# A different table of ordering offsets for the instruction streams of a two-layer attention and feed-forward kernel

## The chip, the core and the metric

The kernel runs on one core of one Trainium2 chip. The metric is the device time of one execution in microseconds (us), the median of three runs. One profiled execution of the kernel before is at hand too, with a trace of every instruction. TensorE is PE below (its weight loads PEld), VectorE is DVE, ScalarE is ACT, GpSimd is POOL, and SyncE, which issues most DMAs, is SP.

## What is computed

The input x has 2048 rows (tokens) of 640 numbers in bf16. Four residual steps follow one another: attention layer A, feed-forward layer B, and the same two again with the same weights.

```python
def _A_ref(x, wq, wk, wv, wo, beta):          # H=32 heads of Dh=20, N=4 segments of L=512 rows
    q, k, v = x @ wq, x @ wk, x @ wv          # cut into heads and segments
    phi = lambda t: jnp.where(t > 0, t + 1.0, jnp.exp(t))
    g = _sigmoid(beta).reshape(1, H, 1, 1)
    M, z = 0, 0                               # memory, one matrix and one vector per head
    for s in range(N):
        logits = jnp.einsum('bhqd,bhkd->bhqk', qs, ks) * scale + mask      # causal in the segment
        a_dot = jnp.einsum('bhqk,bhkd->bhqd', _softmax(logits), vs)
        num = jnp.einsum('bhld,bhde->bhle', phi(qs), M)
        den = jnp.einsum('bhld,bhd->bhl', phi(qs), z)[..., None] + 1e-06
        outs.append(g * num / den + (1.0 - g) * a_dot)
        M = M + jnp.einsum('bhld,bhle->bhde', phi(ks), vs)
        z = z + jnp.einsum('bhld->bhd', phi(ks))
    return concat(outs) @ wo

def _B_ref(x, w1, w2):                        # w1 640 x 1728, w2 1728 x 640
    return jnp.maximum(x @ w1, 0) @ w2

x = x + _A_ref(_layernorm(x), wq, wk, wv, wo, beta)
x = x + _B_ref(_layernorm(x), w1, w2)
x = x + _A_ref(_layernorm(x), wq, wk, wv, wo, beta)
x = x + _B_ref(_layernorm(x), w1, w2)
```

## The kernel before

**Tiling.** x stays on chip as 16 blocks of 128 rows (`x_sb`). All work goes by segments of four such blocks, eight in all: four of the first pass through A and B, called phases 0 to 3 below, and four of the second, phases 4 to 7. In each segment a layer norm by DVE and POOL (statistics L785 and L787, the power -1/2 L801, normalization L831) writes `xn_tok`; a DMA transposes it into `xnT` (`turn`, L804, issued at L807). PE multiplies `xnT` with wq, wk and wv (`proj_one`, `proj_v`), five products of contraction 128 for each output of 128 x 512 or 128 x 320. The helper `group` gives each product in two forms: one matmul over the whole array (L764) or four matmuls of 32 columns each, quarters (L767). The planner picks the form by the tiling that PE is in.

The sums in PSUM (`ps`) are copied out by ACT or DVE, whichever the planner finds free sooner (`evac`, L491; `settle`, L971 on DVE and L972 on ACT for q and k). q and k (`stg`) are then spilled to HBM (`spill`, L1060, `scr`) and read back with four heads spread over the array's rows (`fill`, L1109, `pad`). Scores (L1293) run in rounds of small matmuls on four row groups, ACT takes the exponential of each 128 x 1024 result (L1357), POOL masks the diagonal blocks (L1369), and PE applies the result to v in four column groups (`apply`, L1389), whose output is copied out at L1399 (`otu`) and transposed to `otk` by DMA. `phi_` (L1136 on DVE, L1138 on ACT, L1139 on DVE) computes phi(q) and phi(k) from `stg` once the block is spilled, into `phs`; `turn_k` transposes phi(k) by DMA (`phk`); `mem_write` multiplies it with v (L1230, again as full matmuls or as quarters, the latter with only the columns of the heads that the quarter holds, except in the first of each group). `out_proj` multiplies with wo and adds to x (L1511), `ln_b` is the second layer norm, `ffn` multiplies with w1, applies the relu (L1586 on DVE, L1587 on ACT), multiplies with w2 and adds to x (`residual`, L1606); `ffn_rest` (L1564) does the 64 columns of w1 that don't fill a block. `late_loads` brings in the weights for the first pass and later parts of x (L641) on SP.

**Order.** Nothing here is ordered by hand. The work is written as 39 generators, called streams, each of which yields its instructions in its own order, such as `scores` (number 0), `spill` (13), `turn_k` (19), `mem_write` (20), `proj_one` (29 and 30), `ffn` (32) and `late_loads` (38). A planner (`Sched.run`) keeps a model of when every engine is free and when every result is there. At each step it looks at the next instruction of each stream and records the one with the least key. Each engine, and SP's DMA queue with it, later executes its instructions in the recorded order, with waits on semaphores for what they depend on. The key is (L407):

```python
key = (round(start + late + SHIFT.get(self.place(n, st[1]), 0)),
       0.5 if op.urgent else prio, self.rank[id(st[1])], n)
```

`start` is the modelled start in ns. `late` (`_late`, L348) adds what a PE instruction would be short of a fixed distance behind what it waits for, once the first score rounds are done: 400 ns behind another engine, 1000 ns behind a DMA's landing. `SHIFT` is a table of offsets in ns, and `place` (L260) says which entry holds:

```python
def place(self, n, gen):
    k = self.made.get(id(gen), 0)
    return n, self.phase.get(id(gen), 0), sum(k >= x for x in (6, 20, 60))
```

An entry's name is thus the number of the stream, the phase that it is in (0 to 7), and how many instructions it has recorded in that phase: 0 for under 6, 1 for under 20, 2 for under 60, 3 beyond. A negative offset makes the planner record the instruction earlier than its modelled start, a positive one later. Offsets change the order in which instructions of different streams are recorded. With the order can change which engine copies a sum out, and which form a product has, since both are picked when it is recorded. An order in which a DMA is recorded earlier on SP also moves whatever stands behind it: SP waits in order, for example in `turn` until the block has been written, and in `fill` until the spilled block has landed.

## Time and profile before

| what | value |
|---|---|
| median of three runs | 552.99 us (550.38, 552.99, 553.38) |
| the profiled execution | 550.77 us, of which the span of instructions 548.3 us |
| PE busy | 540.1 us, 99%, 10283 matmuls |
| DVE, ACT, POOL busy | 424.7 us, 409.9 us, 196.8 us |
| granted TensorE clock | 1.0 |
| HBM traffic | 20.57 MB read, 12.85 MB written |

The span runs from the first to the last instruction of the profiled execution; the time around it is 2.5 us. An engine's busy time is the sum over its instructions, without waits. L12 means line 12 of the kernel; in `group`, `turn` and other helpers all callers share a line and are told apart by their operands. In a row of the trace that lists instructions in order, the first number is the start in us from the span's start, the second the time until the last of the xN instructions in that row ended, and a bracket gives the idle time before it with what ended it. `SPq` is SP's DMA queue, where the second number is the time for issuing.

### The profile page before, as it was taken

To read this page: it belongs to the slowest core of one execution; us is meant where nothing else is said; L and a number is where in the kernel's file an instruction comes from. 1 tells how busy PE (TensorE), PEld (TensorE's weight loads), DVE (VectorE), ACT (ScalarE), POOL (GpSimd) and SP (SyncE) were. 2 spreads that over 40 slices of the span, in tenths; PEclk is the share of its full clock that TensorE was granted. 3 is DMA by queue.
4 is the path that set the end of the run, shared out by engine and by line. 5 is a ranking of instruction groups with operands and counts; after the bars stand their busy time and mean duration, and the time that the engine had idled before them with its cause. 6 is when DMAs were issued, how large, how long until landed. Compare 5 with 4: busy or idle time off the path is not lost.

```text
span 548.3 us, 22987 instructions
## 1 busy us (share of the span) xinstructions
PE 540.1 (99%) x10283; PEld 309.9 (57%) x10283; DVE 424.7 (77%) x1060; ACT 409.9 (75%) x522; POOL 196.8 (36%) x305
## 2 busy tenths in 40 slices
PE   8999999999999999999999999999999999999997
PEld 7434465455554555545465554665456655657766
DVE  4999898798889789987798887989688877637102
ACT  6899979899878898788888878886787776551140
POOL 2655533343444334343344444334333322301000
PEclk9999999999999999999999999999999999999999
DMA  8799789845635326375384614571265611340401
GB/s 272 189 231 259 162 179 203 222 86 105 164 83 89 78 39 163 78 114 77 115 144 114 110 31 140 115 126 26 52 179 102 122 34 28 80 83 15 88 4 51
DMA packets 133476, 62.36 MB, mean 114 GB/s; under 512 B 112258, under 2 KB 123266, under 8 KB 133378
## 3 DMA queue, kind: packets, MB, share of 16 engines
q1 hardware_dynamic: 132832, 60.38, 50.8%
q8 instruction: 81, 1.33, 1.0%
q10 hardware_dynamic: 546, 0.52, 0.3%
q14 instruction: 17, 0.14, 0.1%
HBM read 20.57 MB, written 12.85 MB: 61 GB/s over the span
## 4 chain that ended last, share of the span: by engine, by line
PE 89%; DVE 4%; DMA 4%; POOL 1%; ACT 1%; SPq 1%; issue 1%
PE ps L767 48%; PE ps L764 22%; PE ps L1293 9%; PE ps L1389 6%; PE ps L1172 2%; DMA scr<-stg 1%; DMA x_sb<-in_A_x_dram 1%; PE ps L1230 1%; DMA otk<-otu 1%; PE ps L1564 1%; ACT PT L1357 1%; DVE stats L785 1%; POOL PT L1369 1%; SPq L615 0%; POOL rstd L801 0%
## 5 line engine op out<-in xcount | busy, mean ns | idle before, releaser
L1357 ACT ACTIVATE PT<-ps 128x1024 bf16<-128x1024 f32 x320 | 309.3, 1023 | 61.6 <-PE ps L1293 57.6
L1369 POOL TENSOR_SCALAR_AFFINE_SELECT PT<-PT 128x512 bf16<-128x512 bf16 x256 | 169.9, 681 | 247.6 <-ACT PT L1357 247.6
L767 PE MATMUL ps<-xnT,w_r 128*32 128x512 bf16 x1856 | 110.9, 379 | 0.0
L767 PE MATMUL ps<-w_r,hT 128*32 128x320 bf16 (+1 forms) x1876 | 72.7, 295 | 0.0
L767 PEld LDWEIGHTS ps<-xnT,w_r 128*32 128x32 bf16 x1856 | 46.7, 97 | 44.6 <-issue 5.0
L1293 PE MATMUL ps<-pad 20*128 20x512 bf16 (+3 forms) x1024 | 63.3, 301 | 0.0
L764 PE MATMUL ps<-w_r,hT 128*128 128x320 bf16 x376 | 60.3, 300 | 0.0
L1606 DVE TENSOR_TENSOR x_sb<-x_sb,ps 128x320 bf16<-128x320 bf16 (+1 forms) x65 | 30.7, 475 | 37.8 <-PE ps L767 35.6
L785 DVE BATCH_NORM_STATS2 stats<-x_sb 128x6 f32<-128x320 bf16 x124 | 55.2, 474 | 3.9 <-DMA x_sb<-in_A_x_dram 3.3
L767 PEld LDWEIGHTS ps<-w_r,hT 128*32 128x32 bf16 x1876 | 47.9, 97 | 12.4 <-issue 1.6
L1293 PEld LDWEIGHTS ps<-pad 20*128 20x128 bf16 x1024 | 17.8, 92 | 51.1 <-issue 25.0
L764 PEld LDWEIGHTS ps<-w_r,hT 128*128 128x128 bf16 x376 | 34.7, 98 | 17.5 <-issue 5.0
L1587 ACT ACTIVATE hT<-ps 128x512 bf16<-128x512 f32 x52 | 31.1, 598 | 17.9 <-PE ps L767 17.3
L1586 DVE TENSOR_SCALAR hT<-ps 128x512 bf16<-128x512 f32 x52 | 35.3, 680 | 11.7 <-PE ps L767 9.0
L1511 DVE TENSOR_TENSOR x_sb<-x_sb,ps 128x320 bf16<-128x320 bf16 x64 | 30.1, 478 | 15.5 <-PE ps L767 12.1
L801 POOL TENSOR_TENSOR rstd<-lnU,mhalf 128x2 f32<-128x2 f32 (+2 forms) x27 | 21.0, 778 | 56.2 <-DVE lnU L797 42.8
L1389 PE MATMUL ps<-PT,v_aug 128*21 128x128 bf16 (+3 forms) x896 | 40.3, 300 | 0.0
L1399 DVE CAST otu<-ps 128x512 bf16<-128x512 f32 x50 | 34.1, 683 | 7.9 <-PE ps L1389 7.6
L971 DVE CAST stg<-ps 128x512 bf16<-128x512 f32 x42 | 28.5, 683 | 8.4 <-PE ps L767 7.1
L1483 DVE TENSOR_TENSOR o_sb<-otk,rden 128x320 bf16<-128x320 bf16 x62 | 33.9, 571 | 0.6
L831 DVE TENSOR_SCALAR xn_tok<-x_sb,mv,rstd 128x640 bf16<-128x640 bf16 x60 | 29.8, 519 | 3.4 <-POOL rstd L801 3.4
L1138 ACT ACTIVATE stg<-stg 128x512 bf16<-128x512 bf16 x50 | 31.6, 631 | 0.4 <-DVE rtmp L1136 0.4
(113 smaller groups left out, 706.7 us busy)
## 6 DMA issues: line engine op xcount, KB each, us to landing
pad<-scr SPq DMA_DIRECT2D x124, 80.0 KB
scr<-stg SPq DMA_DIRECT2D x34, 256.0 KB, 2.6
out_dram<-x_sb SPq DMA_DIRECT2D x15, 160.0 KB, 2.2
w_r<-in_B_w_dram SPq DMA_DIRECT2D x10, 216.0 KB, 3.8
w_r<-in_B_w_dram SPq DMA_DIRECT2D x13, 160.0 KB, 2.9
x_sb<-in_A_x_dram SPq DMA_DIRECT2D x10, 160.0 KB, 3.3
scr<-w_r SPq DMA_DIRECT2D x5, 256.0 KB, 4.0
wv_r<-in_A_wv_dram SPq DMA_DIRECT2D x1, 800.0 KB, 7.7
```

What stands on the lines that cost most here:

```text
L764: return e.matmul(view(dst.ap, b), a, b, start=(k == 0), stop=(k == last))
L767: return e.matmul(view(dst.ap[rows], b), part, b, start=(k == 0), stop=(k == last))
L785: tk = yield dve(320, 1, lambda e, c2=c2: e.bn_stats(stats6[:, t, c2, :], x_sb[:, t, c2 * 320:(c2 + 1) * 320]), xt)
L1138: te = yield act(512, lambda e, q=q: e.activation(q, q, ACT.Exp), [tr] + p, psum=False)
L1293: fns.append([(lambda e, z=z, j=j, hh=hh, N=N, o=o, sl=sl, q=hh % 2: e.matmul(slot.ap[:, q, o:o + N], sl.ap[32 * hh:32 * hh + DH, z, 0, 12 ...
L1357: tx = yield act(1024, lambda e, dst=dst, src=src: e.activation(dst, src, ACT.Exp, scale=SCALE), sc + pw)
L1369: tm = yield pool(600.0, lambda e, reg=reg: e.affine_select(out=reg, in_=reg, pattern=[[0, 4], [1, 128]], compare_op=ALU.is_ge, fill=0.0, ...
L1389: fns.append((lambda e, OD, j=j, hh=hh: e.matmul(OD.ap[32 * hh:32 * hh + DH + 1, 128 * j:L], VAUG[vx(a, s)][:, j, 4 * g + hh, :], pt.ap[:, ...
L1399: te = yield evac(L, 1, lambda e: e.tensor_copy(dst, OD.ap), lambda e: e.activation(dst, OD.ap, ACT.Copy), [tk] + OTU[0].tks)
L1483: to = yield dve(320, 1, lambda e, z=z, dst=dst: e.tensor_tensor(dst, av[:, z, :, :, 0:DH], rd.ap[:, z].to_broadcast([128, NJ, 4, DH]), AL ...
L1586: th = yield evac(512, 1, lambda e: e.tensor_scalar(hT[:, dc, :], bk.ap[:, :], 0.0, None, ALU.max), lambda e: e.activation(hT[:, dc, :], b ...
L1587: lambda e: e.activation(hT[:, dc, :], bk.ap[:, :], ACT.Relu), [tk] + HT.tks)
```

## The change

The table `SHIFT` is replaced; nothing else differs. It had 265 entries and has 278. 201 names are in both, 10 of them with the same value. Instructions, tiles, buffers, transfers and the planner's rules stay, so that every difference between the two kernels is one of order, of the form of a product (full or quarters) or of the engine that copies a sum out of PSUM. The new table came out of a search over the planner's model in which landing times of DMAs were varied. The lines behind the table have numbers higher by two afterwards. Of the diff, the entries of some streams follow, with the values before and after (a dash is no entry, which counts as 0):

```
stream (number)      (phase, count): before -> after
causal (2)           (0,0): -100 -> -700   (0,1): -663 -> -700   (0,2): -1075 -> -700   (1,0): 400 -> 4050   ...
turn_pair (5)        (0,0): -5225 -> -6362   (1,0): 500 -> -1500   (3,0): -1988 -> -6000   ...
out_proj (8, 9)      (8,7,0): 3000 -> 200   (8,7,1): 3500 -> -   (8,7,2): 3000 -> 100   (9,7,0..2): 1000 -> -50   ...
fill (12)            (1,0): 2274 -> 1462   (2,0): 5175 -> -50   (2,1): -3537 -> -50   ...
spill (13)           (0,0): -888 -> -400   (1,0): 200 -> -   (2,0): 7413 -> 4300   (3,0): -50 -> 425   ...
turn_k (19)          (0,0): 500 -> -200   (1,0): - -> -200   (2,0): 500 -> -   (5,0): -3850 -> -400   ...
mem_write (20)       (2,0): -200 -> -100   (4,1): 225 -> -900   (6,1): -700 -> -1600   ...
proj_first (28)      (0,0): 475 -> -850   (0,1): -400 -> 50   (0,2): -200 -> -
proj_v (31)          (1,1): -6000 -> -875   (2,0): - -> -2500   (7,1): -5350 -> -   (7,2): - -> -2000   ...
ffn (32)             (7,0): 100 -> 3000   (7,1): -7500 -> 3000   (7,2): -7500 -> 3000   (7,3): 500 -> 2925   ...
late_loads (38)      (0,0): -12 -> -   (0,1): 175 -> -100   (0,2): 3087 -> 2400
```

and as lines of the code, shortened:

```diff
 SHIFT = {
-    (0, 0, 0): -12, (0, 1, 1): -26, (0, 2, 0): -50, (0, 3, 0): -50, (1, 0, 0): -312, (1, 0, 1): -1663,
...
+    (37, 0, 0): 300, (37, 0, 1): 2250, (38, 0, 1): -100, (38, 0, 2): 2400,
 }
```

## The prediction

> **What bounds the kernel now.** I read the page first, then PE's busy time by stretches, then who PE waited for, then single rows in order of time.

> ```profile
> span 548.3 us, 22987 instructions
> PE 540.1 (99%) x10283; PEld 309.9 (57%) x10283; DVE 424.7 (77%) x1060; ACT 409.9 (75%) x522; POOL 196.8 (36%) x305
> ```

> TensorE is the bound: 540.1 of 548.3 us. The next view splits the span into stretches (columns: length, then busy time and instructions of each engine, granted clock, DMA share).

> ```profile
> 0.00:27.40 27.40, 24.54 (x220) 16.75 (x221) 19.60 (x57) 19.38 (x40) 12.50 (x31) 1.00 0.82 231
> 27.40:54.80 27.40, 25.05 (x390) 10.69 (x388) 25.94 (x60) 25.98 (x29) 14.37 (x23) 1.00 0.97 245
> 82.20:520.90 438.70, 438.70 (x8739) 250.20 (x8740) 350.17 (x865) 335.49 (x414) 157.73 (x234) 1.00 0.48 100
> 520.90:548.30 27.40, 24.55 (x680) 17.12 (x668) 4.05 (x9) 5.61 (x10) 0.00 (x0) 1.00 0.09 28
> ```

> Between 82 and 521 us PE is never idle. It is idle 2.35 us in the second stretch. There DVE is busy 25.94 of 27.40 us, ACT 25.98, and the DMA engines 0.97 of the time, so three resources besides PE are full. The first and last stretch lose 2.86 and 2.85 us, at the ramp and behind the last matmul. Both orders record PE alike up to about 16 us and in the last 30 us, so those losses stay.

> ```profile
> PE ps L767 <- DVE w_r L971: 0.6, 1, 0.6
> ```

> This is the largest of PE's waits behind the ramp (us, times, longest): a projection's products for a bank that DVE is to evict. It falls between 32 and 50 us, as do smaller ones behind other evictions of DVE and a mask of POOL.

> **Is a busy PE a full PE?** Read start to start:

> ```profile
> 117.70 0.32 PE L767 MATMUL ps<-w_r,hT 128*32 128x320 bf16 x4
> 117.84 1.25 PE L767 MATMUL ps<-xnT,wk_r 128*32 128x512 bf16 x20
> 118.92 0.72 PE L1389 MATMUL ps<-PT,v_aug 128*21 128x512 bf16 x16
> ...
> 120.59 1.24 PE L764 MATMUL ps<-xnT,wk_r 128*128 128x512 bf16 x5
> 121.67 1.11 PE L764 MATMUL ps<-w_r,hT 128*128 128x320 bf16 x7
> ...
> 124.32 0.65 PE L1230 MATMUL ps<-v_aug,phk 128*32 128x147 bf16 x48
> 124.86 0.40 PE L1389 MATMUL ps<-PT,v_aug 128*21 128x512 bf16 x4
> ```

> Five products of width 512 take 117.84 to 118.92 as quarters and 120.59 to 121.67 as full matmuls: 0.216 us each, either way. Four quarters of width 320 take 0.14 us (117.70 to 117.84). So the tiling that the order picks for a product costs nothing. [...]

> **The change part by part.** Only offsets of recording keys differ. I counted both built orders, engine by engine.

> *PE's work.* Matmuls go from 10283 to 10328, but products do not change: eight full products more for every 32 quarters fewer. Changes of tiling are 322 in both. One kind gets cheaper: in the memory write, 18 full matmuls become 18 groups of four quarters, most of them with narrower columns. A full write of 12 takes 0.81 us and one of 12 groups 0.54 us (124.32 to 124.86 above):

> ```profile
> 80.98 0.97 PE L1230 MATMUL ps<-v_aug,phk 128*128 128x147 bf16 x12
> 81.79 0.70 PE L764 MATMUL ps<-wv_r,hT 128*128 128x320 bf16 x4
> ```

> So 18 x (67 - 45) ns = **-0.4 us**, on the bound, with nothing to hide it.

> *An eviction that moves from DVE to ACT.* A 128x512 eviction of a projection, on DVE at 23.7 us before, stands on ACT now, between L1138 and the exponentials behind it.

> ```profile
> 23.61 1.94 ACT L1357 ACTIVATE PT<-ps 128x1024 bf16<-128x1024 f32 x2
> 25.43 0.63 ACT L1138 ACTIVATE stg<-stg 128x512 bf16<-128x512 bf16 x1
> 26.37 1.94 ACT L1357 ACTIVATE PT<-ps 128x1024 bf16<-128x1024 f32 x2 [0.30 <-PE ps L1293]
> ```

> It takes about 0.6 us, an estimate from L1138's row, and delays the exponentials at 23.61. ACT idles 0.30 us before 26.37, which absorbs half. The score round that waits for those exponentials now stands one width-320 product later (0.14 us). Bounds 0 and +0.6; I take **+0.15**, nearer the row of the idle time. Its place on DVE falls free, in the stretch where PE waits on DVE.

> *The other waits of 27 to 55 us.* Score rounds, masks and evictions keep their PE distance to within 0.3 us, except where the 0.8 us write shrinks. I take **0**; bounds -2.35 (all idle time gone) and +1.2 (two new waits like the one of 0.6).

> *The last layer norm.* In the last 60 us out_proj's last groups move in among the products of the previous feed-forward. The last transposed block now waits for a residual add with only 224 quarter matmuls, 56 x 0.136 = 7.6 us, recorded between the add's matmul and the reader. Before, it was 336 quarters or 11.4 us.

> ```profile
> 504.11 0.21 DVE L787 BATCH_NORM_AGGREGATE mv<-stats 128x2 f32<-128x12 f32 x1
> ...
> 504.60 0.82 POOL L801 TENSOR_TENSOR rstd<-lnU,mhalf 128x2 f32<-128x2 f32 x1 [2.57 <-DVE lnU L797]
> 505.14 0.88 DVE L1606 TENSOR_TENSOR x_sb<-x_sb,ps 128x320 bf16<-128x320 bf16 x2
> 505.94 0.80 DVE L831 TENSOR_SCALAR xn_tok<-x_sb,mv,rstd 128x640 bf16<-128x640 bf16 x2
> 507.42 2.00 SPq L807 DMA_TRANSPOSE xnT<-xn_tok  x1
> ...
> 515.45 0.72 PE L1564 MATMUL ps<-xnT,w_r 128*32 128x256 bf16 x20
> xnT<-xn_tok SPq DMA_TRANSPOSE x26, 3.7
> phk<-phs SPq DMA_TRANSPOSE x12, 4.0
> scr<-stg SPq DMA_DIRECT2D x34, 256.0 KB, 2.6
> ```

> The chain now: add 0.5 and its start 0.2, aggregate to end of rstd 1.3 (504.11 to 505.42), two normalizations 0.8, queue 0.1, landing 3.7 (median): 6.6 us. The spare falls from 515.45 - 507.42 - 3.7 = 4.3 us to 7.6 - 6.6 = 1.0 us. **0**, bound +1; if a landing takes over 4.7 us, every us beyond it is lost.

> *Spills behind weights.* Before, five spills of one segment went out in a batch; then came the loads of w2 and the pad fills without a stop.

> ```profile
> 86.98 3.80 SPq L1060 DMA_DIRECT2D scr<-stg  x5
> ...
> 103.70 1.60 SPq L1109 DMA_DIRECT2D pad<-scr  x4
> 114.00 1.26 SPq L807 DMA_TRANSPOSE otk<-otu  x1
> 118.85 1.42 SPq L807 DMA_TRANSPOSE phk<-phs  x1
> 121.05 0.28 DVE L1136 TENSOR_SCALAR rtmp<-stg 128x512 bf16<-128x512 bf16 x1
> ```

> Now two go ahead of the loads. The third and fourth follow the last load, each with a fill behind it that holds SP until the spill lands. From about 104 us that is twice 2.6 us, with four fills of 0.4 us between: SP reaches otk at about 111.5, before its 114.00. The fifth stands behind the phk transpose: issued at 119.3 to 120.3, landed 2.6 us later at 121.9 to 122.9. Its reader L1136 is recorded later too, some 4 us of PE work further on, so not before about 122.9. **0**; bounds 0 and +2.

> Sum against the profiled execution's own 550.77 us (span 548.3 and 2.5 around it): -0.4 + 0.15 = -0.25, so 550.5.

> *From this execution to the median.* The runs were 550.38, 552.99 and 553.38; the profiled one stands 2.2 us below the median. Order and engine times are fixed, so I put that to landings, which in the trace come just ahead of their readers in places:

> ```profile
> 384.29 1.33 SPq L807 DMA_TRANSPOSE xnT<-xn_tok  x1
> 388.03 1.25 PE L767 MATMUL ps<-xnT,wq_r 128*32 128x512 bf16 x20
> ```

> At 388.03 the reader starts 3.7 us after the issue, which is the median landing itself; at 124.32 the phk reader starts 5.5 us after the issue at 118.85. Counted in PE work from the last matmul the block depends on to its reader, the first grows from 6.1 to 7.5 us in the new order (22 products of 512, three score rounds and one apply before; 13 of 512, 17 of 320, three rounds and two applies now). The second shrinks from 7.7 to 7.4. One place better, one slightly worse: I give the new order half of the 2.2 us, bounds none and all. 552.99 - 0.25 - 1.1 = **551.6 us**.

> **The rivals.** *A, the forecast*, 551.6: its own range 550.2 to 553. Chance 0.45.

> *B, faster*: most of the 2.35 us idle of 27 to 55 us goes, because DVE has an eviction less ahead of the wait of 0.6 us, and late landings are covered. 550.77 - 0.25 - 2.35 = 548.2 if all, 549 to 550 if half. For it: the shortest distances grow. Against: the idle time has several causes, and ACT, equally full, gets what DVE loses. Chance 0.27.

> *C, slower*: the fifth spill lands late. L1136 then blocks DVE in order, and with it the evictions behind, whose PSUM banks PE needs. It decides once the spill needs over about 2.6 us. At 4.0, the phk median, DVE stands 1.0 to 1.4 us; at 5 us over 2. With a last landing over 4.7 us and no landing gain, 552.99 - 0.25 + 2 + 0.5 = 555.2, from 553.5 to 557. [...] Chance 0.28, of which 0.2 lies beyond 555.8.

> **How the numbers follow.** 0.5% is 2.8 us, about what a measurement of this kernel can tell from no change. Under 550.2 is B, 0.27; over 555.8 is 0.2; the rest 0.53. The range 548.5 to 556.2 cuts the far ends of B and C, about 0.1 each.

> **What would show it.** L1230 with 22 full matmuls; PE idle near 2.35 us from 27 to 55 us; the reader after the last transpose without a wait on DMA; L1136 near 123 us without idle time behind a spill. Wrong, if PE is idle anywhere from 82 to 521 us for over 1 us, or if the second stretch is full.

## The result, and the profile after

The new order is slower: 554.22 us (median of 22 executions, 551.96 to 557.99) against 551.56 us (22 executions, 549.45 to 553.38), a ratio of 1.0052 with an interval of 1.0039 to 1.0065, or 2.7 us. The profiled execution took 554.71 us. L1295 of the new kernel is the L1293 of before.

The head of its page and its stretches (columns as in the prediction):

```profile
span 552.4 us, 23077 instructions
PE 541.9 (98%) x10328; PEld 309.4 (56%) x10328; DVE 427.3 (77%) x1054; ACT 411.2 (74%) x528; POOL 195.4 (35%) x305
27.40:54.80 27.40, 24.76 (x364) 10.26 (x364) 25.48 (x57) 25.84 (x29) 16.58 (x27) 1.00 1.02 235
54.80:82.20 27.40, 25.80 (x277) 13.41 (x269) 24.71 (x70) 22.16 (x29) 9.90 (x16) 1.00 0.90 175
82.20:520.90 438.70, 438.10 (x8744) 249.58 (x8745) 354.26 (x866) 337.01 (x420) 158.21 (x238) 1.00 0.49 101
```

PE's idle time from 27 to 55 us is 2.64 us, near the 2.35 of before. The next stretch has changed. Before, PE was idle for 0.12 us in it; now for 1.60 us, and the DMA share has gone from 0.79 to 0.90. The row of before:

```profile
54.80:82.20 27.40, 27.28 (x268) 15.11 (x268) 24.97 (x72) 23.41 (x34) 12.15 (x18) 1.00 0.79 171
```

PE's waits name the cause, and its rows in order of time give the place, in the new order:

```profile
PE ps L1295 <- DMA pad<-scr: 1.5, 1, 1.5
...
62.80 0.38 PE L766 MATMUL ps<-hT,wq_r 128*128 128x512 bf16 x1
64.69 0.40 PE L1295 MATMUL ps<-pad 20*128 20x512 bf16 x4 [1.51 <-DMA pad<-scr]
```

A score round waits for the fill of `pad`. SP's queue shows what stands ahead of that fill, first in the new order, then in the old (the kernel before, profiled again, with its PE row):

```profile
51.17 1.85 SPq L809 DMA_TRANSPOSE hT<-xn_tok  x1
53.07 2.48 SPq L647 DMA_DIRECT2D w_r<-in_B_w_dram  x4
55.59 0.44 SPq L1062 DMA_DIRECT2D scr<-w_r  x1
57.05 1.40 SPq L809 DMA_TRANSPOSE otk<-otu  x1
58.55 3.94 SPq L1111 DMA_DIRECT2D pad<-scr  x8
```

```profile
50.07 1.40 SPq L807 DMA_TRANSPOSE hT<-xn_tok  x1
51.51 1.67 SPq L645 DMA_DIRECT2D w_r<-in_B_w_dram  x3
53.23 0.43 SPq L1060 DMA_DIRECT2D scr<-w_r  x1
55.52 1.76 SPq L807 DMA_TRANSPOSE otk<-otu  x1
57.38 3.48 SPq L1109 DMA_DIRECT2D pad<-scr  x9
61.77 0.39 PE L1293 MATMUL ps<-pad 20*128 20x512 bf16 x4 [0.34 <-DMA pad<-scr]
```

In the old order three loads of w1 stand between the transpose and the spill, in the new one four, and the batch ends 2.4 us later (56.03 against 53.66), while the fill is issued only 1.2 us later. From the fill's issue to PE's start it takes 6.1 us now and 4.4 us in the old order, where the wait was 0.34 us at most: the old order had no time to spare here. The new order's second profile, at full clock throughout, shows the same without the slow stretch described next: there the batch ends at 55.37 us, the fill is issued only 0.3 us later than in the old order, and it takes 5.7 us to PE's start.

```profile
57.70 4.16 SPq L1111 DMA_DIRECT2D pad<-scr  x8
63.44 0.39 PE L1295 MATMUL ps<-pad 20*128 20x512 bf16 x4 [1.16 <-DMA pad<-scr]
```

One more row differs. The granted clock of this execution falls to half for some 3.4 us (windows of 2 us of the new order; the clock is the last column but two):

```profile
8.00:10.00 2.00, 1.46 (x18) 1.29 (x16) 1.27 (x4) 0.28 (x1) 0.74 (x2) 0.74 1.09 345
10.00:12.00 2.00, 2.00 (x21) 2.00 (x20) 0.34 (x1) 1.11 (x4) 0.00 (x0) 0.50 1.07 361
12.00:14.00 2.00, 2.00 (x27) 1.89 (x25) 1.28 (x3) 1.12 (x4) 0.00 (x0) 0.91 0.90 300
```

Up to there both orders are the same on every engine, so this profile alone cannot say whether the clock belongs to the change.

### The profile page after: what moved, and what is told of

Read it like the earlier page. It is cut to its first block, busy times and chain, and to the rows that moved or that the text cites. A ratio compares the mean times of both kernels' runs of the same rounds, so it can differ in the third digit from the quotient of the medians.

```text
span 552.4 us, 23077 instructions
## 1 busy us (share of the span) xinstructions
PE 541.9 (98%) x10328; PEld 309.4 (56%) x10328; DVE 427.3 (77%) x1054; ACT 411.2 (74%) x528; POOL 195.4 (35%) x305
## 3 DMA queue, kind: packets, MB, share of 16 engines
q8 instruction: 81, 1.33, 1.0%
## 4 chain that ended last, share of the span: by engine, by line
PE 86%; DVE 7%; DMA 4%; ACT 1%; POOL 1%; issue 1%; SPq 0%
PE ps L769 48%; PE ps L766 21%; PE ps L1295 8%; PE ps L1391 5%; PE ps L1174 2%; DMA otk<-otu 2%; DVE stats L787 1%; DMA pad<-scr 1%; DVE otu L1401 1%; PE ps L1232 1%; DVE phs L1141 1%; PE ps L1566 1%; ACT PT L1359 1%; DMA scr<-stg 1%; DVE o_sb L1485 1%
## 5 line engine op out<-in xcount | busy, mean ns | idle before, releaser
L769 PE MATMUL ps<-xnT,w_r 128*32 128x512 bf16 x1824 | 108.8, 379 | 0.0
L1295 PE MATMUL ps<-pad 20*128 20x512 bf16 (+3 forms) x1024 | 63.4, 301 | 1.6 <-DMA pad<-scr 1.5
L766 PE MATMUL ps<-w_r,hT 128*128 128x320 bf16 x384 | 62.7, 300 | 0.0
L787 DVE BATCH_NORM_STATS2 stats<-x_sb 128x6 f32<-128x320 bf16 x124 | 55.0, 475 | 3.3 <-DMA x_sb<-in_A_x_dram 2.5
L769 PEld LDWEIGHTS ps<-w_r,hT 128*32 128x32 bf16 x1844 | 45.9, 97 | 14.7 <-issue 2.5
L1295 PEld LDWEIGHTS ps<-pad 20*128 20x128 bf16 x1024 | 17.8, 92 | 52.4 <-ACT PT L1359 23.7
L1589 ACT ACTIVATE hT<-ps 128x512 bf16<-128x512 f32 x55 | 32.9, 598 | 17.6 <-PE ps L769 17.1
L1401 DVE CAST otu<-ps 128x512 bf16<-128x512 f32 x52 | 35.4, 682 | 7.7 <-PE ps L1391 7.6
L1588 DVE TENSOR_SCALAR hT<-ps 128x512 bf16<-128x512 f32 x49 | 33.1, 681 | 5.5 <-PE ps L769 2.8
L1485 DVE TENSOR_TENSOR o_sb<-otk,rden 128x320 bf16<-128x320 bf16 x62 | 37.1, 622 | 0.3
L769 PE MATMUL ps<-wo_r,oT 128*32 128x320 bf16 x824 | 34.5, 300 | 0.0
L833 DVE TENSOR_SCALAR xn_tok<-x_sb,mv,rstd 128x640 bf16<-128x640 bf16 x60 | 31.8, 558 | 2.8 <-POOL rstd L803 2.5
## 6 DMA issues: line engine op xcount, KB each, us to landing
scr<-stg SPq DMA_DIRECT2D x34, 256.0 KB, 3.0
scr<-w_r SPq DMA_DIRECT2D x5, 256.0 KB, 4.1
```

Of the source, the lines that this page charges most:

```text
L766: return e.matmul(view(dst.ap, b), a, b, start=(k == 0), stop=(k == last))
L769: return e.matmul(view(dst.ap[rows], b), part, b, start=(k == 0), stop=(k == last))
L787: tk = yield dve(320, 1, lambda e, c2=c2: e.bn_stats(stats6[:, t, c2, :], x_sb[:, t, c2 * 320:(c2 + 1) * 320]), xt)
L833: nm = lambda e, bx, t, k: e.tensor_scalar(bx.ap[:, k * D:k * D + D], x_sb[:, t + k, :], mv[:, t + k, 0:1], rstd[:, t + k:t + k + 1], ALU. ...
L1295: fns.append([(lambda e, z=z, j=j, hh=hh, N=N, o=o, sl=sl, q=hh % 2: e.matmul(slot.ap[:, q, o:o + N], sl.ap[32 * hh:32 * hh + DH, z, 0, 12 ...
L1401: te = yield evac(L, 1, lambda e: e.tensor_copy(dst, OD.ap), lambda e: e.activation(dst, OD.ap, ACT.Copy), [tk] + OTU[0].tks)
```

## The experiments

In all but the first two, the planner's choice is replaced by a list. The list holds, for each of the 5065 recorded instructions, its stream, engine, form of product and modelled end, so that an order can be cut and joined or a single instruction moved without disturbing the rest:

```diff
-                key = (round(start + late + SHIFT.get(self.place(n, st[1]), 0)), ...)
-                if best is None or key < best[0]:
-                    best = (key, st, end, start, k, op)
+            lab, k, mode, at = REPLAY[self.step]
+            st = [st for st in self.streams if self.lab(st) == lab and not st[4]][0]
```

Both orders have recorded the same set of instructions at records 413 (39 us), 874 (86 us) and 1577 (157 us), so they can be joined there. Ratios are to the kernel before on the same chip.

**The two kernels again.** No edit.

> The kernel before, unchanged, profiled again. If the slow clock that the changed kernel's profile shows at 9 to 12 us comes by chance in both kernels (up to there their recorded orders are equal on every engine), some of these runs have a mean clock below 1.0 as well, and those are longer by about 1.5 us. If instead only the new order brings it, all of these runs are at 1.0. Ratio to the kernel before: 1.000 plus or minus 0.002.

> The changed kernel, unchanged, profiled again. Theory 1, the fill: PE waits 1 to 2 us at the score round near 62 us for the fill of pad, in this execution too, also at a full clock, and the ratio is 1.005. Theory 2, chance landings: this wait is absent or under 0.3 us, and other waits for landings stand elsewhere. Theory 3, the clock: with a mean clock of 1.0 the excess over the kernel before is under 0.5 us.

Measured: before 550.79 us, ratio 1.0002 (0.9988 to 1.0016); after 554.59 us, 1.0073 (1.0047 to 1.0099), at full clock in the profiled execution, with the wait for `pad` at 1.16 us. Theory 1 holds. The slow clock does come by chance in both kernels, but not equally often: of the executions with a clock on record 14 of 104 of the kernel before had a mean clock below 1.0, and 13 of 26 of the kernel after. In the first 22 of these 26 the median is 553.1 us at full clock and 555.0 us below it. Theory 3 is wrong as the whole cause, since at full clock the new order is still over 2 us longer.

**Which part of the order.**

> The first 874 of 5065 records (up to about 86 us) in the new order, all later ones in the old: both orders have recorded the same set of instructions at that point. Theory 1, the DMA traffic that the new order pushes up to 50 to 60 us and the fill behind it: most of the loss is here, +1.5 to +2.5 us, ratio 1.003 to 1.0045. Theory 2, the landings that the new order spreads over the rest (spills behind weights, the last layer norm): 0 to +0.7 us, ratio 1.000 to 1.0013. Theory 3, the clock: 0.

> The complement, cut at the next point where both orders have recorded the same set: the first 1577 records (up to about 157 us) in the old order, all later ones in the new. Theory 1: 0 to +0.5 us, ratio 1.000 to 1.001, or below 1 by the cheaper memory writes (0.4 us). Theory 2: +1.5 to +2.7 us, ratio 1.003 to 1.005. Theory 3: 0.

> The first 413 of 5065 records (up to about 39 us) in the new order, the rest in the old. The traces so far put the loss in three places: 0.7 us from 23 to 35 us, 1.1 to 1.4 us at the fill near 62 us, 0.6 us near 86 us. Theory 1, the loads of w1 that stand behind the transposes from 44 us on delay the fill: they are recorded after this cut, so only the first place shows, +0.5 to +0.9 us, ratio 1.001 to 1.0016, PE's wait for pad under 0.4 us. Rival, the traffic is already late by 39 us and the fill inherits that: PE's wait for pad stays at 1 us or more, +1.7 us or more, ratio 1.003 or more.

> Old order up to record 413, new order from there to record 874 (39 to 86 us), old order behind. Theory 1: the fill and the place near 86 us show, +1.6 to +2.0 us, ratio 1.003 to 1.0036, with a wait for pad of 1 us or more. Rival: the wait for pad is under 0.4 us, +0.6 us or less, ratio 1.001 or less.

```diff
-REPLAY = new[0:5065]
+REPLAY = new[0:874] + old[874:]                  # early_after
+REPLAY = old[0:1577] + new[1577:]                # late_after
+REPLAY = new[0:413] + old[413:]                  # first_after
+REPLAY = old[0:413] + new[413:874] + old[874:]   # mid_after
```

| new order from record | us | ratio | interval | PE's wait for pad |
|---|---|---|---|---|
| 0 to 874 | 554.76 | 1.0068 | 1.0044 to 1.0091 | 1.4 us |
| 1577 on | 551.49 | 1.0008 | 0.9994 to 1.0022 | none |
| 0 to 413 | 551.39 | 1.0005 | 0.9988 to 1.0022 | none |
| 413 to 874 | 555.44 | 1.0069 | 1.0044 to 1.0095 | 1.0 us |

The new records between 39 and 86 us alone lose as much as the whole new order. The eviction that moved at 23 us and the last layer norm lie outside and cost nothing that can be measured. The spills behind weights stand between 86 and 157 us, which no hybrid has in the new order; that they cost nothing is read from PE's lag (below), which grows there no more than in the old order. The two hybrids that hold the loss are above what was expected (1.003 to 1.0045, and 1.003 to 1.0036). Both also show a wait of PE at 280 us for nothing that the profile names (1.1 and 0.8 us), which neither order alone has; they are therefore upper bounds.

**Is it the transfers ahead of the fill?** Once they are taken away from the new order, once brought into the old.

> The new order with one difference on SP's queue alone: the last three loads of w1 and the fifth spill of the second segment (0.9 MB) go out behind the fills and the transpose of phk at 62 us and not ahead of the fills at 53 to 55 us; their readers come at 75 us and later. Theory 1, these transfers are what the fill queues behind: the fourth piece of pad lands about 3 us after its issue and not 3.4 to 4.8 us, PE's wait for it goes from 1.2 us to under 0.3 us, and the time falls by 1 us against the new order, ratio to the kernel before 1.003 to 1.005. Rival, the fill is late because PE and the engines that feed it are late, and transfers do not matter: the wait stays at 1.2 us, ratio 1.005 to 1.007. A loss elsewhere is possible: the moved transfers then meet the transposes of oT at 66 us, whose reader comes 7 us later.

```diff
 SP's queue, new order, 53 to 63 us
-w1 load 17; w1 loads 18, 19, 20; spill 9; turn_pair 3; fill 22-29; turn_k 2
+w1 load 17; turn_pair 3; fill 22-29; turn_k 2; w1 loads 18, 19, 20; spill 9
```

> The kernel before with two loads of w1 moved on SP's queue as in the new order, nothing else: the first from ahead of a transpose of xn_tok at 43 us to behind the next transpose of otu at 46 us, the fourth from ahead of the second transpose of xn_tok at 49 us to behind it. Theory 1: the wait for pad near 61.6 us goes from 0 to 0.3 us to over 1 us, ratio 1.002 to 1.003. Rival, this needs the other changes of the new order too: wait under 0.5 us, ratio 1.000 to 1.001.

```diff
 SP's queue, old order, 42 to 53 us
-w1 load 14; turn xn; turn_pair 2; w1 loads 15, 16; spill 8; w1 load 17; turn xn; w1 loads 18-20; spill 9
+turn xn; turn_pair 2; w1 loads 14, 15, 16; spill 8; turn xn; w1 loads 17-20; spill 9
```

Without those transfers the wait for `pad` is gone: 553.26 us, ratio 1.0030 (1.0016 to 1.0045), and 1 of 12 executions was below full clock. But the moved megabyte meets the next transposes, and PE waits there (rows of that kernel):

```profile
67.33 0.69 PE L1232 MATMUL ps<-w_r,phk 128*128 128x147 bf16 x8 [0.61 <-DMA phk<-phs]
71.58 1.52 PE L766 MATMUL ps<-wo_r,oT 128*128 128x320 bf16 x10 [0.96 <-DVE stg L973]
```

The second bracket names DVE, whose `stg` had ended by 71.20 us; the transpose of `oT`, issued at 66.59, landed 4.9 us later, at 71.49.

The other way round, two moved loads alone make the old order slower: 552.90 us, ratio 1.0024 (1.0006 to 1.0043), with 7 of 12 executions below full clock. In the profiled one the fill takes longer, but PE was early there:

```profile
56.52 4.12 SPq L1109 DMA_DIRECT2D pad<-scr  x9
61.73 0.40 PE L1293 MATMUL ps<-pad 20*128 20x512 bf16 x4 [0.88 <-DMA pad<-scr]
```

From issue to PE's start that is 5.2 us against 4.4 in the old order. The wait (0.88 us) is a little under the 1 us expected. In these two runs PE's wait for the fill comes and goes with what was issued ahead of it on the same queue: 1.16 to 1.51 us in the new order and none without those transfers, 0 to 0.34 us in the old order and 0.88 us with the two moved loads.

**Moving the loads further back.**

> The new order with one difference on SP's queue: the last four loads of w1 (0.86 MB, read from 90 us on) go out behind the transposes of oT and xn_tok at about 72 us and not at 53 to 55 us; the spill stays. Theory 1, backlog of transfers: the fourth piece of pad lands about 3 us after its issue, PE's wait for it is under 0.3 us, and, other than in the earlier try, no new wait for phk or oT comes at 66 to 70 us; ratio to the kernel before 1.002 to 1.004, by what is left near 86 us and at 30 to 50 us. Rival, the loss only moves to whichever transfer comes next: a new wait of about 1 us between 62 and 85 us, ratio 1.005.

> The kernel above, and on ACT the eviction of v at 85 us ahead of the two exponentials of phi that wait for DVE (it stood behind them). Theory: the two waits of PE near 85 and 87 us, 0.6 us together, go, ratio 0.001 under that of the kernel above. Rival, DVE is the bound there and PE's wait only moves on to the next eviction: no change within 0.2 us.

> The kernel before with the same move of four w1 loads. Theory 1: its fill had no time to spare (PE's wait was 0 and 0.3 us in two traces), so the gain is 0 to 0.5 us, ratio 0.999 to 1.000, with fewer executions at a mean clock below 1.0. Rival, the moved loads get in the way of the spills and fills of 72 to 80 us: ratio 1.001 or more, with PE's wait for pad or phk behind 72 us.

```diff
 SP's queue, new order (in the old one load 17 stands ahead of the first turn xn)
-turn xn; w1 loads 17-20; spill 9; turn_pair 3; fill 22-29; turn_k 2; turn_o 1, 2; turn xn; turn xn; turn_k 3
+turn xn; spill 9; turn_pair 3; fill 22-29; turn_k 2; turn_o 1, 2; turn xn; turn xn; w1 loads 17-20; turn_k 3
 ACT's queue, evict_first besides
-phi exp; phi exp; eviction of v
+phi exp; eviction of v; phi exp
```

All three miss: 554.22 us, 1.0074 (1.0056 to 1.0093); 554.46 us, 1.0083 (1.0054 to 1.0113); 553.81 us, 1.0055 (1.0038 to 1.0072). The wait for `pad` is gone in each, as theory 1 says, but each has a new one of about 2 us near 91 us. The two rivals on moved loads held in that the loss moved on to another transfer; it was `xnT`, though, which neither named, and in the new order it came later than the 62 to 85 us of the rival. In the two new orders the profile names nothing for this wait, but PE starts 0.1 us behind the landing of the same transpose. In the old order with the loads moved, SP's queue and PE show it:

```profile
72.36 2.54 SPq L645 DMA_DIRECT2D w_r<-in_B_w_dram  x4
74.94 2.29 SPq L807 DMA_TRANSPOSE phk<-phs  x1
...
82.65 4.52 SPq L807 DMA_TRANSPOSE xnT<-xn_tok  x2
...
90.77 1.04 PE L1564 MATMUL ps<-xnT,w_r 128*32 128x256 bf16 x20 [2.12 <-DMA xnT<-xn_tok]
92.00:94.00 2.00, 2.00 (x24) 0.64 (x16) 1.77 (x7) 0.63 (x1) 0.00 (x0) 0.50 1.03 385
```

Four loads take 2.5 us of the queue, and what stands behind them goes out later, in the end the transposes of `xnT` for the feed-forward: the second is issued 1.3 us later than in the old order (84.51 against 83.17) and lands 6.2 us behind its issue, not 3.5. Behind the wait the clock is at half (last row, a window of 2 us). The eviction put forward, ahead of one of the two exponentials and not of both, did not help either: PE's wait of 0.16 us for it at 84.7 us went, and one of 0.22 us for another eviction on DVE took its place at 86.4 us, so there the rival that DVE is the bound held.

**What brings the slow clock.**

> The kernel before with three loads of w1 and one spill moved from ahead of a transpose of otu to behind it, so that the fill is issued 1.7 us later; PE is to idle 1.5 to 2.5 us near 62 us. Theory on the clock, an idle PE there brings the slow clock: at least half of the executions have a mean clock of 0.997 or less, and these are 1.5 us longer; in a profile of such an execution the granted clock is half just behind the wait. Rival, the slow clock comes from the first 12 us and by chance: under a quarter of the executions. Ratio 1.003 to 1.006 by the theory, 1.003 to 1.004 by the rival.

```diff
 SP's queue, old order, 52 to 61 us
-w1 loads 18, 19, 20; spill 9; turn_pair 3; fill 22-30
+turn_pair 3; w1 loads 18, 19, 20; spill 9; fill 22-30
```

554.37 us, ratio 1.0067 (1.0049 to 1.0086). The wait is longer than expected, 3.1 us, and 5 of 6 executions are below full clock. The profiled one shows where (PE's row, then windows of 2 us):

```profile
64.24 0.39 PE L1293 MATMUL ps<-pad 20*128 20x512 bf16 x4 [3.12 <-DMA pad<-scr]
64.00:66.00 2.00, 1.76 (x46) 1.31 (x47) 0.23 (x1) 1.33 (x2) 0.00 (x0) 1.00 1.01 122
66.00:68.00 2.00, 2.00 (x13) 0.45 (x12) 1.93 (x6) 1.72 (x3) 0.64 (x1) 0.50 0.34 74
68.00:70.00 2.00, 2.00 (x11) 0.78 (x8) 0.55 (x2) 1.91 (x3) 0.00 (x0) 0.65 0.97 187
```

The clock stays full for almost 2 us behind the wait and is then half for some 3.4 us, which costs 1.7 us of matmuls. So the theory on the clock holds for a wait of this length. In all runs together, executions below full clock were 41 of 76 in kernels with an added wait for `pad` or `xnT` of about 0.9 us or more, and 10 of 72 in the other changed kernels (the one with waits of 0.61 and 0.96 us at 67 and 72 us among these, with 1 of 12). These counts go by the mean clock of an execution and do not say where the dip is. Five profiled executions are below full clock. In three the dip begins 0.3 to 1.8 us behind the long wait (this kernel and the two with moved loads, at 66.00, 91.04 and 93.10 us). In two it lies at 9 to 12 us: the new order's first profile, and the kernel with the eviction put forward (mean clock 0.997), whose own wait of 2.2 us brought none. No profiled execution shows a dip behind a wait for `pad` of 1.5 us or less; that it sits there in half of the new order's executions is inferred from the counts and not shown.

**Taking the wait away by an earlier fill.**

> The new order with the four pieces of the fill that PE waits for near 62 us moved on SP's queue from behind the transpose of otu at 57 us to ahead of it, where SP stood idle for 0.8 to 1 us. Nothing else is moved, no transfer comes later than before by more than 0.5 us. Theory 1, the loss is this wait and the slow clock that it brings: wait for pad 0, a mean clock below 1.0 in under a quarter of the executions, ratio 1.0005 to 1.003, against 1.005 to 1.007 for the new order. Rival, the transfers of this stretch are at their limit and the wait comes back at the next one, as with the moved loads of w1: a new wait of 1 us or more between 57 and 95 us, ratio 1.0045 or more.

> The kernel before with the same move; there SP stands idle for 2 us ahead of that transpose, so it costs nothing on the queue. Theory 1: the fill, which had no time to spare, lands 2 us ahead of its reader; PE's wait for pad 0 and fewer executions below full clock, gain 0.1 to 0.5 us, ratio 0.999 to 1.000. Rival: earlier fills delay the loads and transposes of 55 to 60 us and PE waits there, ratio 1.001 or more.

> The new order with the fill ahead up to record 626 (about 62 us), the old order behind, so without the two waits near 85 and 87 us. If these 0.6 us count in the time: ratio 0.001 under that of the new order with the fill ahead, 0.9995 to 1.0015. Rival, they are absorbed: equal to it within 0.2 us.

```diff
 SP's queue, either order, 53 to 60 us
-spill 9; turn_pair 3; fill 22-25; fill 26-29
+spill 9; fill 22-25; turn_pair 3; fill 26-29
 ahead_old626 besides
+REPLAY = that[0:626] + (old without what that[0:626] holds)
```

```profile
56.18 1.55 SPq L1111 DMA_DIRECT2D pad<-scr  x4
57.77 1.29 SPq L809 DMA_TRANSPOSE otk<-otu  x1
...
62.91 0.40 PE L1295 MATMUL ps<-pad 20*128 20x512 bf16 x4
```

These are rows of the new order with the fill ahead: PE starts without a wait. It took 552.39 us, ratio 1.0033 (1.0015 to 1.0051), 2 of 12 executions below full clock. The upper end of what was expected (1.003) is just passed, and the rival's new wait did not come; the transpose that the fill passed goes out 0.7 us later than in the new order's first profile. The interval overlaps that of the new order (1.0039 to 1.0065), so the gain in time is not shown by this run alone; the executions below full clock, 2 of 12 here and 1 of 12 with the transfers taken away against 13 of 26, point the same way. What is left, 1.7 us by the medians (552.39 against 550.74), is not this wait. With the old order from record 626 on it took 551.77 us, 1.0011 (0.9995 to 1.0027). The same move in the old order gave 550.43 us, ratio 0.9992 (0.9980 to 1.0005), with none of 12 executions below full clock: no gain that can be told from none.

## Why the prediction was wrong

How far PE lags its own work shows where the time goes. This table, worked out from the traces, gives the start of the matmul at a given point of PE's work, less that work (products by their width, and an estimated 0.1 us for each of the 322 changes of tiling in either order: 36 quarters of width 320 begin at 83.94 us in the old order, would end at 85.16 at 0.034 us each, and the round behind them begins at 85.27):

```
PE's work so far, us      30     50     55     70     75    250    500
before, again           7.14  10.15  11.14  11.40  11.43  13.02  15.13
after, again            7.85  11.16  12.99  13.26  13.86  15.45  17.94
after, fill ahead       8.36  11.87  12.46  12.73  13.32  15.22  17.83
the same, old from 626  7.41  10.72  11.43  11.79  11.82  13.53  15.55
```

Against the kernel before, the new order loses 0.7 us up to 30 (some of it chance: the seven other kernels with these records stood there at 7.3 to 8.8), 0.3 from 30 to 50, 0.85 at the fill (50 to 55), 0.6 from 70 to 75 (PE's waits for evictions at 85 to 87 us of the span), 0.4 behind that, and has 0.6 us less work: 2.2 us at full clock; the two spans differ by 2.3 us. Below full clock the executions of the new order are about 1.9 us longer (555.0 against 553.1), and that is half of them instead of one in seven: 0.7 us on average. That makes 2.9 us, where 2.7 us were measured. The fill's own part is 0.85 us, and 1.55 with the clock if the dips sit behind it: about half. The rest is placed by this table; of it only the first part (records up to 413, ratio 1.0005) and the 0.6 us at 85 to 87 us were tried by themselves.

*The failed step is "The other waits of 27 to 55 us".* It priced them at 0 because score rounds, masks and evictions keep their distance in PE work. It looked at engines and not at SP's queue, although its own row gave the DMA engines as 0.97 busy. The loads of w1 in that stretch were not costed at all; only the spills behind w2 at 87 to 122 us were. Two loads that moved behind transposes take away the little that the fill had to spare. The wait that they bring, 1.2 to 1.5 us for `pad`, comes at 62 to 65 us, behind the end of the step: for 55 to 82 us the sum has no term, and the prediction's view of stretches leaves 54.8 to 82.2 us out. Its bound of +1.2 us is of the size of that wait, but by luck, since it was made of waits of DVE's evictions.

*A missing term: the clock.* The prediction read 1.00 in every row and had no rival in which an idle PE costs more than its idle time. In the kernels with an added wait of 0.9 to 3.1 us about half of the executions were below full clock, and in both series of the new order these were 1.6 to 1.9 us longer. Where the dip sits in them is open, as said above.

*From this execution to the median.* The 2.2 us between the profiled execution and the median of three, half of which was given to the new order as a gain of landings, was mostly a chance of three runs: over 22 the kernel before has 551.56 us, 0.8 above its profiled 550.77. And the sign was wrong: the new order scatters more, over 6.0 us against 3.9. Engine times were not fixed either, as that step took them to be: the mean clock was below 1.0 in 14 of 104 executions of the kernel before.

*PE's work, -0.4 us.* Right in kind. By its groups the memory write has 22 full matmuls, as forecast:

```profile
L1232 PE MATMUL ps<-v_aug,phk 128*128 128x147 bf16 x10 | 1.2, 227 | 0.0
L1232 PE MATMUL ps<-v_aug,phk 128*128 128x168 bf16 x4 | 0.8, 233 | 0.0
L1232 PE MATMUL ps<-w_r,phk 128*128 128x147 bf16 x8 | 0.7, 228 | 0.0
```

The count of all PE work falls by 0.6 us. No run measured this gain by itself.

*The eviction, +0.15 us.* It takes 0.61 us on ACT (estimate 0.6), and the order with the new records up to 413, which hold it, is at 1.0005 (0.9988 to 1.0022): nothing that can be measured. The row is of the changed kernel, profiled again:

```profile
23.67 0.61 ACT L974 ACTIVATE stg<-ps 128x512 bf16<-128x512 f32 x1
```

*The last layer norm, 0.* Right: its reader starts without a wait, 4.9 us after the last transpose is issued (same kernel).

```profile
512.80 1.36 SPq L809 DMA_TRANSPOSE xnT<-xn_tok  x1
...
517.73 0.72 PE L1566 MATMUL ps<-xnT,w_r 128*32 128x256 bf16 x20
```

*Spills behind weights, 0.* The price was right, the times were not. From the third and from the fifth spill to the fill behind it SP stands for 4.4 us instead of 2.6, and the reader comes at 126.24 instead of near 123. PE is not held there: from 100 to 150 us of its work its lag grows by 0.5 us, in the old order by 0.6. No run shows the 2 us that rival C added for it.

```profile
106.29 0.59 SPq L1062 DMA_DIRECT2D scr<-stg  x1
110.72 1.44 SPq L1111 DMA_DIRECT2D pad<-scr  x4
...
121.70 0.90 SPq L1062 DMA_DIRECT2D scr<-stg  x1
126.07 1.41 SPq L1111 DMA_DIRECT2D pad<-scr  x4
126.24 0.28 DVE L1138 TENSOR_SCALAR rtmp<-stg 128x512 bf16<-128x512 bf16 x1
```

So rival C had the right side and the right kind, a late landing, but at the wrong place and by another chain: the late spill that it priced cost PE nothing. Rival B's idle time of 27 to 55 us did not shrink, by the row shown first.

Open stays what puts the 0.6 us at 85 to 87 us into the time. The step from 1.0033 to 1.0011 agrees with it, but the intervals overlap, and the one edit aimed at it only moved the wait.

## What to carry to other kernels

Where PE is busy throughout and the DMA queue is full for a stretch, an order must be read on the queue first: for each transfer that PE waits for, take its issue, its landing and its reader, and list what stands ahead of it on the queue in the new order. To relieve such a transfer, move it forward into time in which the queue stands idle: here that took away a wait of 1.2 to 1.5 us, while both ways of moving the loads back delayed what came behind them. A wait of 2 to 3 us on PE should be priced with the clock that it may cost, some 1.7 us here, half of a dip of 3.4 us.

## What the runs showed of the hardware

In three profiled executions a half clock of some 3.4 us follows a wait of PE shorter than that: from 66.00 us behind the wait of 3.12 us (the old order with the fill behind), from 91.04 us behind 2.12 us and from 93.10 us behind 1.98 us (the old and the new order with the moved loads). By kernel, executions below full clock were 5 of 6 with a wait of 3.1 us, 10 of 18 with one of about 2 us, 13 of 26 in the new order with 1.2 to 1.5 us, and 14 of 104 in the kernel before.

With all profiled executions cut by their grids, PE is idle for 2.12, 1.98 and 1.66 us in the step just ahead of these dips; between 12 us and the last matmul no other step has over 1.64 us idle, and none has a dip behind it. Behind the last matmul of the new order's first profile 2.23 us of a step are idle, and half clock follows at 551.66 us. The wait of 2.2 us without a dip was cut by a step's end into 0.58 and 1.63 us. So in these traces the dips stand behind steps in which PE was idle for about half or more (an estimate, from the three dips behind a wait), and where a wait falls on the grid would be the chance in it. In the first 10 us, at the ramp, this border does not hold: dips stand behind steps with 1.47 and 1.55 us idle, and none behind one with 1.71.
